# A planner's costs for TensorE and GpSimd, and the due times that go with them, replaced by another set

## The chip, the core and the metric

The kernel runs on one core of a Trainium2 chip. The metric is the time of one execution in microseconds (us) of device time. Before the change three runs gave 1165.32 us as their median (1164.49 to 1168.14).

## What is computed

Attention over 4 batches of 12 heads (448 positions, 64 numbers a head) with RMS-normalised queries and keys, then two feed-forward layers over its 1792 x 768 output, all in fp32:

```python
q_n, k_n = rmsnorm(q, g_q), rmsnorm(k, g_k)
scores = 1 / sqrt(64) * q_n @ k_n.T                  # per head
attn = exp(scores - max) / (sum + 1e-9)
x = (attn @ v) laid out as (1792, 768)
h = x @ w_in;   x = (h / (1 + exp(-h))) @ w_out      # layer 1, w_in 768 x 2048, w_out 2048 x 768
h = x @ w_in2;  x = max(h, 0) ** 2 @ w_out2          # layer 2, the same sizes
```

The inputs of the layers' weights are 8-byte floats, read as two 4-byte words each.

## The kernel before

**The work.** 24 pairs of heads go through attention one after another. Layer 1 then runs in 8 segments (two halves of the tokens, each with four quarters of the 2048 inner columns), layer 2 in 16 groups of 256 inner columns (two halves of the tokens, 8 groups each; the second half's down projection, line 1568, goes by seven products too). Each fp32 operand is split in two parts, an upper one (a rounded copy, names ending in hi) and a lower one (the difference, names ending in lo), and each product is three matmuls: upper by upper, upper by lower, lower by upper. Line 558 (`lower_part`) makes all lower parts on VectorE or GpSimd, lines 549 and 551 (`upper_part`) the upper ones on ScalarE or VectorE.

**Seven products in place of eight.** But for the first segment, whose up projection is plain (line 1017), an up projection forms 2 x 2 blocks by the scheme of seven products (`seven`, line 1104: a product is 9 matmuls of 128x448). Sums of weights are made for it at lines 1062 and 1081 (`four`), sums of activations at lines 1307 and 1253, and its results are collected from PSUM by `plus` (line 1119, VectorE). Layer 1's down projection is line 1201, its results are taken up at lines 1213 to 1221. Layer 2's down projection is lines 1443 and 1568 (sums of hidden values for it at line 1500, of weights at line 1529), its results are added at line 1462 on VectorE, and at the end of the kernel line 1620 joins the blocks. PSUM has 4 buffers "s" (down projections), 3 buffers "t" and 1 buffer "pv" (up projections).

**What sets the order.** Nothing here is issued in the order in which it is written. Every operation is recorded as a step with the engines that may do it and a time on each. A planner (class `Plan`) then plays the program: at each point it takes the step that can start first, and among those that can start at once the one with the smallest due time (`forward`). Its answer is the order of each engine's instructions and, where a step may run on several engines, the engine. Due times come from a backward pass (`backward`) plus the constants of the table `DUE`, one per kind of step and part of the program ("seg0" and "seg1" are the halves of layer 1; "end0" ends some way ahead of layer 2's second half, "end1" follows). Attention's steps stand at fixed places (`nominal`); only other work that is put between them moves. The chip follows the order, and each instruction still waits for its data by semaphore, so a wrong time in the planner makes an engine wait and never a wrong result.

The times that the change touches: `SWITCH` (line 113, added where TensorE changes between forms of matmul), `pool_t` and `any_t` (lines 475 and 478, GpSimd's time for n elements per partition), `lower_part`'s rate (line 555), four transposes (`turn_q`, line 670, and `turn_e`, line 750), attention's second product (line 807), and `PROD` (line 1040, one product of 9 matmuls). For the layers' SBUF operations a step of `any_t` may go to VectorE or GpSimd: the planner leaves it to the engine that would end it first, and it keeps two such operations from running on both engines at once (the `lock` in `forward`). An upper part (`copy_t`) may go to ScalarE or VectorE by the same rule.

Of the kernel before, what the change touches and what calls it, by code (L numbers as in the profile page):

```python
# [98 lines left out]
class Step:  # L99
# [10 lines left out]
LAG = {"pe": 0.21, "act": 0.13, "dve": 0.12, "pool": 0.12, "sp": 1.9, "none": 0.0}  # L110
SELF = {"pe": 0.0, "act": 0.1, "dve": 0.1, "pool": 0.06, "sp": 1.9, "none": 0.0}
FORM = {"scores": "rows", "attend": "columns"}
SWITCH = 0.16
ENGINES = ("pe", "act", "dve", "pool", "sp", "none")
ROUNDS = 8
AHEAD = 25.0
DUE = {
    "end0": {"acc": 4.25, "down2": -1, "h_hi": 21.25, "h_lo": 3.75, "keep_parts2": -1.25, "load_y": -0.75, "p1_copy": 3.75, "prod": 0.25, "square": 1, "u_sum": -0.5, "w_hi2": -6, "w_lo2": -0.75, "w_sum": -0.75, "y_hi": 5.25, "y_lo": 4.25, "y_sum": -3.5},
    "end1": {"acc": 2, "down2": -11.25, "h_hi": 16, "h_lo": 2.5, "h_sum": -39.5, "join": 18, "keep_parts2": -11.75, "load_parts2": -2.25, "load_word2": 1.75, "load_y": 0.5, "p1_copy": 0.5, "prod": 2, "square": 21.25, "store": -1.25, "u_sum": -1, "w_hi2": 4.25, "w_sum": -4.5, "y_lo": -3, "y_sum": 2.5},
    "now": {"ident": 5.75, "swap_pools": -0.5},  # L120
    "seg0": {"add": -0.5, "down": 3, "g_hi": 0.5, "g_lo": 0.75, "keep": 10.25, "load_raw": -6, "load_y": 0.5, "low": 1, "magnitude": -2, "merge": -6, "out1": -1, "p1_copy": 4, "part": 0.5, "prod": 4.75, "silu": 0.5, "store_y": -1, "u_sum": 2.75, "up": 2.5, "w_hi": 4.5, "w_lo": 6.25, "w_sum": -2, "y_hi": 0.75, "y_lo": 1, "y_sum": 2},
    "seg1": {"add": -4.25, "down": -4.5, "g_hi": 2.25, "g_lo": 5, "keep2": 45.25, "load_raw2": 6, "load_word": -5.5, "load_y": -0.75, "low2": -1.5, "magnitude2": -3, "merge2": -4.5, "p1_copy": -6.25, "part": -3.75, "prod": -3.25, "silu": -5.75, "store_y": 7, "u_sum": 2.25, "w_hi": 1.75, "w_lo": 1, "w_sum": -3, "y_hi": 10, "y_lo": 0.75, "y_sum": 2.5},
}


# [280 lines left out]
def kernel(  # L406
# [65 lines left out]
    def dve_t(n, rate=960.0, lock=False):  # L472
        return {"dve": (0.07 + n / rate, None, lock)}

    def pool_t(n, rate=474.0):
        return {"pool": (0.145 + n / rate, None, True)}

    def any_t(n, rate=474.0):
        return {**dve_t(n, 960.0, True), **pool_t(n, rate)}

    def copy_t(n):
# [70 lines left out]

        step(kind, when, copy_t(n), copy, reads=reads, writes=writes)

    def lower_part(kind, when, o, a, h, n, reads, writes, rate=474.0):

        step(
            kind, when, any_t(n, rate), lambda e: engine(e).tensor_tensor(o(), a(), h(), ALU.subtract),  # L558
            reads=reads, writes=writes,
        )  # L560

    def prepare(i):
# [88 lines left out]
        for n in range(2):  # L651
            n32 = sa([CP, NCH, 2, D], F32, "n")
            step(
                "norm", at, any_t(W2, 600.0),
                lambda e, n=n, n32=n32: engine(e).tensor_tensor(
                    n32.ap.rearrange("p c h d -> p h c d"),
                    qk.ap[:, n].rearrange("p (h c) d -> p h c d", h=2),
                    y.ap[:, n].rearrange("p (h c) -> p h c", h=2).unsqueeze(3).to_broadcast([CP, 2, NCH, D]),
                    ALU.mult),
                reads=[y, (qk, n)], writes=[n32],  # L660
            )
            plan.fix(i, "norm", j=n, at="dve" if i < 2 else "pool")
            pt = psum("t")

            def turn(e, n32=n32, pt=pt):
                for c in range(NCH):
                    nc.tensor.transpose(  # L667
                        pt.ap[:, c * CP:(c + 1) * CP], n32.ap[:, c].rearrange("p h d -> p (h d)"), ident.ap)

            step("turn_q", at, pe_t(0.384), turn, reads=[n32, ident], writes=[pt])  # L670
            plan.fix(i, "turn_q", j=n)

            def upper(e, n=n, pt=pt):
                o, a_ = T.ap[:, n, 0], pt.ap[:, :S]
                if n:
                    nc.scalar.activation(o, a_, AF.Copy, scale=G.ap)  # L676
                else:
                    nc.scalar.copy(o, a_)

            def lower(e, n=n, pt=pt):  # L680
                o, a_, h_ = T.ap[:, n, 1], pt.ap[:, :S], T.ap[:, n, 0].bitcast(F32)
                if n:
                    nc.vector.scalar_tensor_tensor(o, a_, G.ap, h_, ALU.mult, ALU.subtract)
                else:
                    nc.vector.tensor_tensor(o, a_, h_, ALU.subtract)

            step("q_hi", at, act_t(S, 0.08 if n else 0.0), upper, reads=[pt, G], writes=[(T, (n, 0))])
            plan.fix(i, "q_hi", j=n)
            step("q_lo", at, dve_t(S), lower, reads=[pt, G, (T, (n, 0))], writes=[(T, (n, 1))])
            plan.fix(i, "q_lo", j=n)  # L690
# [16 lines left out]
    def weigh(i, T):  # L707

        PT = [sa([CP, NB8, CT, CP], F32, "PT") for _ in range(NCH // CT)]
        sums = sb([CP, 2, NCH], F32, "sum", 3)  # L710
        for c in range(NCH):
            at = ("pair", i, c)
            E = sa([CP, 2, S], F32, "E")
            pts = [psum("s"), psum("s")]

            def scores(e, c=c, pts=pts):
                for k_, (a, b_) in enumerate(((0, 0), (0, 1), (1, 0))):
                    for j in range(2):
                        r = slice(j * D, (j + 1) * D)
                        nc.tensor.matmul(  # L720
                            pts[j].ap[:CP, :S], T.ap[r, 0, a, c * CP:(c + 1) * CP], T.ap[r, 1, b_],
                            start=(k_ == 0), stop=(k_ == 2),
                        )

            step("scores", at, pe_t(0.606), scores, reads=[(T, (n, a)) for n in range(2) for a in range(2)], writes=pts)
            plan.fix(i, "scores", c)
            for j, pt in enumerate(pts):
                mx = sa([CP, 1], F32, "mx", 6)
                step(
                    "row_max", at, {"dve": (0.535, None, False)},  # L730
                    lambda e, pt=pt, mx=mx: nc.vector.tensor_reduce(  # L731
                        mx.ap, pt.ap[:CP, :S], AX.X, ALU.max, negate=True),
                    reads=[pt], writes=[mx],
                )
                plan.fix(i, "row_max", c, j)
                step(
                    "exp", at, {"act": (0.62, None, False)},
                    lambda e, j=j, c=c, pt=pt, mx=mx, E=E: nc.scalar.activation(  # L738
                        E.ap[:, j], pt.ap[:CP, :S], AF.Exp, bias=mx.ap, accum_out=sums.ap[:, j, c:c + 1]),
                    reads=[pt, mx], writes=[(E, j), (sums, (j, c))],  # L740
                )
                plan.fix(i, "exp", c, j)
                pe = psum("t")

                def turn(e, j=j, pe=pe, E=E):
                    for m in range(NCH):
                        nc.tensor.transpose(  # L747
                            pe.ap[:CP, m * CP:(m + 1) * CP], E.ap[:, j, m * CP:(m + 1) * CP], ident.ap)

                step("turn_e", at, pe_t(0.384), turn, reads=[(E, j), ident], writes=[pe])  # L750
                plan.fix(i, "turn_e", c, j)
                copy_step(
                    "e_copy", at, ECOPY[c][j], lambda c=c, j=j: PT[c // CT].ap[:, j * NCH:(j + 1) * NCH, c % CT, :],
                    lambda pe=pe: pe.ap[:CP, :S].rearrange("p (m t) -> p m t", t=CP), S, [pe], [(PT[c // CT], (c % CT, j))],
                )
                plan.fix(i, "e_copy", c, j)
        return PT, sums

    def attend(i, vr, PT, sums):
# [32 lines left out]
        for c2, pt in enumerate(PT):  # L792

            def products(e, c2=c2, pt=pt):
                for m in range(NCH):
                    for j in range(2):
                        nc.tensor.matmul(  # L797
                            pv.ap[j * D:(j + 1) * D, c2 * CT * CP:(c2 + 1) * CT * CP],
                            vr.ap[:, j * NCH + m, :],
                            pt.ap[:, j * NCH + m].rearrange("p c t -> p (c t)"),  # L800
                            start=(m == 0),
                            stop=(m == NCH - 1),
                            skip_group_check=True,
                        )

            step(
                "attend", at, pe_t(1.456), products,
                reads=[vr] + [(pt, (c, j)) for c in range(CT) for j in range(2)], writes=[(pv, c2)],
            )
            plan.fix(i, "attend", c2)  # L810
# [226 lines left out]
    FD = 2  # L1037
    halves = {}
    W3 = HC * P
    PROD = 9 * 0.2065  # L1040

    def view(b, a, c):

# [641 lines left out]
```

## Time and profile before

| what | value |
|---|---|
| median of three runs | 1165.32 us |
| the profiled execution, its own time | 1167.08 us |
| its span, first to last instruction | 1165.3 us |
| TensorE busy | 1147.8 us (99% of the span) |
| VectorE busy | 939.3 us (81%) |
| ScalarE busy | 632.3 us (54%) |
| GpSimd busy | 287.9 us (25%), 507 instructions |
| DMA | 202 GB/s over the span |
| mean granted TensorE clock | 0.994 of 2.4 GHz |

Busy times overlap: the engines run side by side. PE is TensorE's matmuls, PEld its weight loads, DVE is VectorE, ACT ScalarE, POOL GpSimd, SP the engine that issues the DMAs. A matmul counts as busy from its start to its last result, so two that follow each other overlap, and a stream of them is read from the distance of their starts. In the chain of waits (the work that ended last, followed back from the last instruction) the time of a piece of TensorE's work is therefore also the time that the stream took.

### The profile page before, as it was taken

Reading aid. Unit: us, or ns where it says so; the run is one execution under the profiler, and the core shown is the slowest. Engines: PE = TensorE matmul, PEld = TensorE weight load, DVE = VectorE, ACT = ScalarE, POOL = GpSimd, SP = SyncE. Lnnn points to the kernel's source line nnn. Section 1 sums busy time; section 2 is a strip of 40 time slices with the busy share of each in tenths; the row PEclk is TensorE's granted clock in tenths of the full one; section 3 lists DMA queues with packets and bytes.
Section 4 is the critical chain, followed back from the end, with each engine's and each line's share of the span. In section 5 each row is a group of like instructions: output and inputs, shape, how many; then the busy total and the mean of one; then the engine's idle time right before and its main releaser. Section 6 shows DMA issues by size and latency. Waiting matters only on the chain.

```text
span 1165.3 us, 19244 instructions
## 1 busy us (share of the span) xinstructions
PE 1147.8 (99%) x6817; PEld 1018.8 (87%) x6817; DVE 939.3 (81%) x1685; ACT 632.3 (54%) x1290; POOL 287.9 (25%) x507
## 2 busy tenths in 40 slices
PE   7999999998999999999999999999999999999998
PEld 5777777777999999999999999999998999999997
DVE  7888888886876868996878698588888976888876
ACT  5999999985554444555535353543433535333321
POOL 4566676632000101210111021001121120122220
PEclk8999999999999999999999999999999999999999
DMA  6566768578855564778776849977777696555444
GB/s 175 94 103 115 105 109 111 99 125 175 275 167 185 172 212 133 263 236 273 244 238 209 272 145 329 337 271 261 286 264 260 217 378 230 177 176 190 164 163 135
DMA packets 142064, 235.22 MB, mean 202 GB/s; under 512 B 32016, under 2 KB 105744, under 8 KB 141968
## 3 DMA queue, kind: packets, MB, share of 16 engines
q1 hardware_dynamic: 141728, 233.80, 67.2%
q8 instruction: 54, 0.88, 0.3%
q14 instruction: 42, 0.34, 0.1%
q10 hardware_dynamic: 240, 0.20, 0.1%
HBM read 157.58 MB, written 76.37 MB: 201 GB/s over the span
## 4 chain that ended last, share of the span: by engine, by line
PE 91%; DVE 4%; ACT 2%; DMA 1%; issue 1%; SPq 0%; POOL 0%; ACTq 0%; DVEq 0%; POOLq 0%
PE t L1104 22%; PE s L1201 20%; PE s L1443 11%; PE pv L1104 9%; PE t L747 7%; PE pv L797 7%; PE s L720 6%; PE s L1568 6%; PE t L1017 2%; PE t L667 2%; DMA raw<-in_moe_w_out_dram 1%; DVE gg L1462 1%; DVE w L558 1%; DVE g L1119 0%; DVE g L1500 0%
## 5 line engine op out<-in xcount | busy, mean ns | idle before, releaser
L1201 PE MATMUL s<-gg,w 128*128 128x448 f32 x1152 | 240.4, 367 | 0.0
L1201 PEld LDWEIGHTS s<-gg,w 128*128 128x128 f32 x1152 | 216.2, 188 | 19.8 <-DVE g L1213 0.3
L1119 DVE TENSOR_TENSOR g<-t,g 128x448 f32<-128x448 f32 x180 | 108.8, 619 | 63.9 <-PE t L1104 53.1
L1443 PE MATMUL s<-w,gh 128*128 128x384 f32 (+1 forms) x564 | 143.0, 334 | 2.1 <-DVE gg L1462 1.1
L738 ACT ACTIVATE E<-s,mx 112x448 f32<-112x448 f32 x192 | 122.9, 653 | 13.7 <-ACT xf L537 7.9
L731 DVE TENSOR_REDUCE mx<-s 112x1 f32<-112x448 f32 x192 | 107.4, 611 | 14.4 <-PE s L720 14.1
L1462 DVE TENSOR_TENSOR gg<-s,gg 128x384 f32<-128x384 f32 (+1 forms) x197 | 102.6, 547 | 18.1 <-PE s L1443 17.7
L558 DVE TENSOR_TENSOR w<-W,w 128x768 fp32r<-128x768 f32 (+1 forms) x123 | 111.7, 917 | 4.2 <-ACT w L549 3.3
L1443 PEld LDWEIGHTS s<-w,gh 128*128 128x128 f32 x564 | 101.8, 188 | 4.0 <-DVE gg L1462 1.9
L1104 PE MATMUL t<-yb,w 128*128 128x448 f32 x468 | 103.1, 367 | 0.2 <-DVE w L558 0.2
L747 PEld LDWEIGHTS t<-ident,E 112*112 112x112 f32 x768 | 73.8, 134 | 32.5 <-issue 19.1
L549 ACT CAST w<-W 128x768 fp32r<-128x768 f32 (+1 forms) x74 | 54.9, 744 | 83.8 <-PE s L1201 31.9
L747 PE MATMUL t<-ident,E 112*112 112x112 f32 x768 | 94.7, 266 | 1.2 <-ACT E L738 1.2
L1368 ACT ACTIVATE g<-g 128x448 f32<-128x448 f32 x48 | 27.7, 578 | 124.6 <-DVE g L1119 124.1
L1443 PE MATMUL s<-w,gl 128*128 128x384 f32 (+1 forms) x282 | 94.3, 335 | 0.3 <-POOL gl L558 0.3
L1104 PEld LDWEIGHTS t<-yb,w 128*128 128x128 f32 x468 | 87.6, 188 | 8.1 <-DVE w L558 0.5
L797 PE MATMUL pv<-PT,vv 112*64 112x224 f32 x768 | 83.0, 359 | 0.1
L720 PE MATMUL s<-T 64*112 64x448 f32 x576 | 73.8, 388 | 1.3 <-ACT T L676 1.2
L1104 PE MATMUL pv<-xb,w 128*128 128x448 f32 x324 | 72.4, 367 | 0.0
L539 DVE COPY PT<-t 112x448 f32<-112x448 f32 x96 | 59.1, 618 | 11.6 <-PE t L747 11.5
L797 PEld LDWEIGHTS pv<-PT,vv 112*64 112x64 f32 x768 | 51.0, 136 | 20.0 <-ACT xf L537 0.3
L1104 PEld LDWEIGHTS pv<-xb,w 128*128 128x128 f32 x324 | 60.7, 188 | 5.5
(168 smaller groups left out, 2213.1 us busy)
## 6 DMA issues: line engine op xcount, KB each, us to landing
raw<-in_moe_w_in_dram SPq DMA_DIRECT2D x32, 768.0 KB
raw<-in_moe_w_out_dram SPq DMA_DIRECT2D x24, 512.0 KB
raw<-in_moe_w_out_dram SPq DMA_DIRECT2D x16, 768.0 KB
su<-w SPq DMA_DIRECT2D x16, 768.0 KB
w<-su SPq DMA_DIRECT2D x16, 768.0 KB
xf<-y SPq DMA_DIRECT2D x48, 224.0 KB
xf<-x SPq DMA_DIRECT2D x39, 224.0 KB
ki<-W SPq DMA_DIRECT2D x16, 384.0 KB
```

The source lines that it names most:

```text
L558: kind, when, any_t(n, rate), lambda e: engine(e).tensor_tensor(o(), a(), h(), ALU.subtract),
L720: nc.tensor.matmul(pts[j].ap[:CP, :S], T.ap[r, 0, a, c * CP:(c + 1) * CP], T.ap[r, 1, b_], start=(k_ == 0), stop=(k_ == 2),)
L731: lambda e, pt=pt, mx=mx: nc.vector.tensor_reduce(mx.ap, pt.ap[:CP, :S], AX.X, ALU.max, negate=True),
L738: lambda e, j=j, c=c, pt=pt, mx=mx, E=E: nc.scalar.activation(E.ap[:, j], pt.ap[:CP, :S], AF.Exp, bias=mx.ap, accum_out=sums.ap[:, j, c:c ...
L747: nc.tensor.transpose(pe.ap[:CP, m * CP:(m + 1) * CP], E.ap[:, j, m * CP:(m + 1) * CP], ident.ap)
L797: nc.tensor.matmul(pv.ap[j * D:(j + 1) * D, c2 * CT * CP:(c2 + 1) * CT * CP], vr.ap[:, j * NCH + m, :], pt.ap[:, j * NCH + m].rearrange("p ...
L1104: nc.tensor.matmul(pt.ap[:, :S], w_()[:, c0 + c, :], view(b, a, c)(), start=(start and c == 0 and k == 0), stop=(c == HC - 1 and k == 2), ...
L1119: lambda e: nc.vector.tensor_tensor(o.ap, pt.ap[:, :S], a.ap, ALU.add),
L1201: nc.tensor.matmul(pt.ap[:, :S], w_()[:, f, :], gg.ap[:, k, a, f, :], start=(f == 0 and n == 0), stop=(f == HQ - 1 and n == 2),)
L1443: nc.tensor.matmul(pt.ap[:, :en], g.ap[:, fi, c0:c0 + P], w_()[:, 0, e0:e0 + en], start=(n == 0), stop=(n == 5),)
L1462: "acc", at, dve_t(n), lambda e: nc.vector.tensor_tensor(o(), pt.ap[:, :n], o(), ALU.add),
L1568: nc.tensor.matmul(pt.ap[:, :NH], a[i][0](m), b[j][0](), start=(start and k == 0), stop=(k == 2), skip_group_check=True,)
```

## The change

Six times of the planner are changed, and the table `DUE` is replaced as a whole; nothing else differs. No operation is added or left out. The numbers of instructions on TensorE (6435) and of DMAs stay; some steps that have a choice move between VectorE, ScalarE and GpSimd.

```diff
-SWITCH = 0.16
+SWITCH = 0.13
...
-    "end0": {"acc": 4.25, "down2": -1, "h_hi": 21.25, "h_lo": 3.75, ...
+    "end0": {"down2": -1.5, "h_hi": 50.5, "h_lo": -0.75, "keep_parts2": 4.25, ...
...
-    def pool_t(n, rate=474.0):
-        return {"pool": (0.145 + n / rate, None, True)}
-
-    def any_t(n, rate=474.0):
+    def pool_t(n, rate=415.0):
+        return {"pool": (0.1 + n / rate, None, True)}
+
+    def any_t(n, rate=415.0):
...
-    def lower_part(kind, when, o, a, h, n, reads, writes, rate=474.0):
+    def lower_part(kind, when, o, a, h, n, reads, writes, rate=415.0):
...
-            step("turn_q", at, pe_t(0.384), turn, reads=[n32, ident], writes=[pt])
+            step("turn_q", at, pe_t(0.406), turn, reads=[n32, ident], writes=[pt])
...
-                step("turn_e", at, pe_t(0.384), turn, reads=[(E, j), ident], writes=[pe])
+                step("turn_e", at, pe_t(0.406), turn, reads=[(E, j), ident], writes=[pe])
...
-                "attend", at, pe_t(1.456), products,
+                "attend", at, pe_t(1.512), products,
...
-    PROD = 9 * 0.2065
+    PROD = 9 * 0.2028
```

How the order moves, at three places. Over the whole program GpSimd has 19 instructions fewer (512 to 493), VectorE 6 more, ScalarE 13 more; among the moved ones are 9 upper parts of weights (128x768) that go from VectorE to ScalarE. TensorE's order is the same up to the end of the first segment's up projection.

**ScalarE, at the end of attention.** W and raw are a weight tile and the 8-byte words that it is made from (lines 920 and 925 read raw), g<-t at line 1029 is the first SiLU of layer 1, which empties a buffer "t" of PSUM. Before:

```order
L537 COPY xf<-pv 128x448
L920 ACTIVATE W<-raw 128x512
L925 ACTIVATE raw<-raw 128x512
L1029 ACT_TABLE_LOAD
L1029 ACTIVATE g<-t 128x448
L549 CAST gg<-g 128x448
L549 CAST w<-W 128x512
L1029 ACTIVATE g<-t 128x448
```

Now:

```order
L537 COPY xf<-pv 128x448
L549 CAST w<-W 128x768
L920 ACTIVATE W<-raw 128x512
L925 ACTIVATE raw<-raw 128x512
L1029 ACT_TABLE_LOAD
L1029 ACTIVATE g<-t 128x448 x2
L549 CAST gg<-g 128x448
L920 ACTIVATE W<-raw 128x512
```

An upper part of weights has come ahead, and the second SiLU follows the first at once. The two reads of raw still stand ahead of the first SiLU.

**TensorE, where the fourth segment's down projection meets the next up projection.** s<-gg is the down projection, t and pv are products of the up projection with the activations yb, xb, xc, gh. Before:

```order
L1201 MATMUL s<-gg,w 128x448 x12
L1104 MATMUL t<-yb,w 128x448 x18
L1104 MATMUL t<-xb,v 128x448 x9
L1201 MATMUL s<-gg,w 128x448 x24
L1104 MATMUL pv<-xb,w 128x448 x9
L1104 MATMUL t<-xc,w 128x448 x9
L1104 MATMUL t<-xb,w 128x448 x9
L1104 MATMUL t<-yb,w 128x448 x9
```

Now:

```order
L1201 MATMUL s<-gg,w 128x448 x144
L1104 MATMUL pv<-gh,w 128x448 x2
...
L1104 MATMUL t<-yb,w 128x448 x18
L1104 MATMUL t<-xb,v 128x448 x9
L1104 MATMUL pv<-xb,w 128x448 x9
L1104 MATMUL t<-xc,w 128x448 x9
L1104 MATMUL t<-xb,w 128x448 x9
```

All 144 matmuls of the down projection now stand ahead of the next segment's first product; before, 24 of them stood between its fourth and its fifth product.

**GpSimd, in layer 2's first half.** gl is a lower part of the hidden values, v and w<-W are lower parts of weights, xf a sum of activations; the numbers count buffers in the order in which the planner issues them. Before:

```order
L558 TENSOR_TENSOR gl_10288<-g_10233,gh_10251 128x448
L558 TENSOR_TENSOR gl_10288<-g_10263,gh_10251 128x448
L558 TENSOR_TENSOR v_10311<-W_10267,v_10311 128x384
L558 TENSOR_TENSOR w_10324<-W_10308,w_10324 128x768
L558 TENSOR_TENSOR gl_10549<-g_10530,gh_10534 128x448
L1253 TENSOR_TENSOR xf_10757<-xf_10757,xf_10772 128x448
L558 TENSOR_TENSOR gl_10851<-g_10828,gh_10833 128x448
```

Now:

```order
L558 TENSOR_TENSOR gl_10006<-g_9822,gh_9993 128x448
L558 TENSOR_TENSOR w_10103<-W_9887,w_10103 128x768
L558 TENSOR_TENSOR w_10333<-W_10307,w_10333 128x768
L558 TENSOR_TENSOR yb_10584<-xf_10070,yb_10584 128x448
L1253 TENSOR_TENSOR xf_10757<-xf_10757,xf_10771 128x448
```

Of four operations that stood together around buffer number 10300 one is left, and a second lower part of 128x768 has come. From the first to the last matmul of layer 2's first half GpSimd has 15 of these operations where it had 27.

## Rows read from the trace of the kernel before

**Rows 1.** The page: the span, busy time by engine, and the chain by engine.

```profile
span 1165.3 us, 19244 instructions
...
PE 1147.8 (99%) x6817; PEld 1018.8 (87%) x6817; DVE 939.3 (81%) x1685; ACT 632.3 (54%) x1290; POOL 287.9 (25%) x507
...
PE 91%; DVE 4%; ACT 2%; DMA 1%; issue 1%; SPq 0%; POOL 0%; ACTq 0%; DVEq 0%; POOLq 0%
```

**Rows 2.** Weight loads' waits, whole span: waited for, us in total, times, longest.

```profile
PEld t L1017 <- ACT g L1029: 3.4, 1, 3.4
```

**Rows 3.** The chain of waits, 262 to 290 us: start, us, what.

```profile
269.79 10.34 DMA raw<-in_moe_w_out_dram
...
282.71 0.55 ACT g L1029
...
283.31 6.72 PE t L1017 x24
```

**Rows 4.** Stretches of 2 us: busy time by engine, PEclk is the granted clock.

```profile
284.00:286.00 2.00, 2.00 (x8) 1.81 (x8) 2.00 (x3) 1.63 (x3) 1.22 (x1) 0.67 1.06 386
286.00:288.00 2.00, 2.00 (x7) 1.74 (x7) 2.00 (x5) 0.56 (x1) 0.00 (x0) 0.50 1.07 284
```

**Rows 5.** The chain of waits, whole span: two streams of 126 matmuls.

```profile
306.78 26.04 PE s L1201 x126
...
583.30 25.53 PE s L1201 x126
```

**Rows 6.** Two stretches of layer 1, in order PE, PEld, DVE, ACT, POOL, clock.

```profile
288.50:511.50 223.00, 223.00 (x1081) 202.52 (x1080) 181.61 (x313) 110.65 (x185) 20.31 (x14) 1.00 0.64 202
515.00:735.00 220.00, 220.00 (x1087) 203.59 (x1086) 170.73 (x284) 107.37 (x170) 30.74 (x22) 1.00 0.75 250
```

**Rows 7.** Weight loads' waits, 288 to 735 us.

```profile
PEld s L1201 <- DVE g L1213: 0.3, 1, 0.3
PEld t L1104 <- DVE g L1119: 0.2, 1, 0.2
```

**Rows 8.** Weight loads' waits, 735 to 990 us.

```profile
PEld s L1443 <- DVE gg L1462: 1.9, 2, 1.5
PEld s L1568 <- DVE part L558: 1.8, 2, 1.1
PEld s L1443 <- POOL gl L558: 0.6, 1, 0.6
PEld t L1104 <- DVE w L558: 0.5, 1, 0.5
PEld pv L1104 <- DVE w L558: 0.5, 1, 0.5
```

**Rows 9.** The timeline of POOL and of DVE around 879 us.

```profile
878.24 1.83 POOL L558 TENSOR_TENSOR w<-W,w 128x768 fp32r<-128x768 f32 x1 [0.35 <-ACT w L549]
...
876.46 0.55 DVE L1062 TENSOR_TENSOR W<-W 128x384 f32<-128x384 f32 x1
...
878.29 2.20 DVE L1081 TENSOR_TENSOR W<-W 128x384 f32<-128x384 f32 x1
```

**Rows 10.** The timeline of PE there, with the idle time before and its releaser.

```profile
881.01 0.61 PE L1443 MATMUL s<-w,gh 128*128 128x384 f32 x2 [1.13 <-DVE gg L1462]
```

**Rows 11.** Layer 2's first half as one stretch.

```profile
735.00:960.00 225.00, 223.09 (x1183) 211.91 (x1182) 183.15 (x306) 94.92 (x168) 36.56 (x27) 1.00 0.77 280
```

**Rows 12.** Groups by line and shape: upper parts of 128x768 on DVE and on ACT.

```profile
L551 DVE CAST w<-W 128x768 fp32r<-128x768 f32 x43 | 26.4, 614 | 9.2 <-PE pv L1104 4.1 <-PE s L1201 4.0
...
L549 ACT CAST w<-W 128x768 fp32r<-128x768 f32 x43 | 35.9, 834 | 57.0 <-PE s L1201 18.0 <-DVE W L1081 12.6 <-PE s L1443 9.4
```

**Rows 13.** Weight loads' waits, 990 us to the end.

```profile
PEld s L1443 <- DVE gh L551: 1.2, 1, 1.2
PEld s L1568 <- ACT part L549: 1.1, 4, 0.3
```

**Rows 14.** The last piece of the chain of waits.

```profile
1161.65 0.36 DVE gg L1462
```

More of the change, by code (lines that the diff above doesn't have):

```diff
@@ L117 @@
 DUE = {
-    "end0": {"acc": 4.25, "down2": -1, "h_hi": 21.25, "h_lo": 3.75, "keep_parts2": -1.25, "load_y": -0.75, "p1_copy": 3.75, "prod": 0.25, "square": 1, "u_sum": -0.5, "w_hi2": -6, "w_lo2": -0.75, "w_sum": -0.75, "y_hi": 5.25, "y_lo": 4.25, "y_sum": -3.5},
-    "end1": {"acc": 2, "down2": -11.25, "h_hi": 16, "h_lo": 2.5, "h_sum": -39.5, "join": 18, "keep_parts2": -11.75, "load_parts2": -2.25, "load_word2": 1.75, "load_y": 0.5, "p1_copy": 0.5, "prod": 2, "square": 21.25, "store": -1.25, "u_sum": -1, "w_hi2": 4.25, "w_sum": -4.5, "y_lo": -3, "y_sum": 2.5},
@@ L120 @@
-    "now": {"ident": 5.75, "swap_pools": -0.5},
-    "seg0": {"add": -0.5, "down": 3, "g_hi": 0.5, "g_lo": 0.75, "keep": 10.25, "load_raw": -6, "load_y": 0.5, "low": 1, "magnitude": -2, "merge": -6, "out1": -1, "p1_copy": 4, "part": 0.5, "prod": 4.75, "silu": 0.5, "store_y": -1, "u_sum": 2.75, "up": 2.5, "w_hi": 4.5, "w_lo": 6.25, "w_sum": -2, "y_hi": 0.75, "y_lo": 1, "y_sum": 2},
-    "seg1": {"add": -4.25, "down": -4.5, "g_hi": 2.25, "g_lo": 5, "keep2": 45.25, "load_raw2": 6, "load_word": -5.5, "load_y": -0.75, "low2": -1.5, "magnitude2": -3, "merge2": -4.5, "p1_copy": -6.25, "part": -3.75, "prod": -3.25, "silu": -5.75, "store_y": 7, "u_sum": 2.25, "w_hi": 1.75, "w_lo": 1, "w_sum": -3, "y_hi": 10, "y_lo": 0.75, "y_sum": 2.5},
+    "end0": {"down2": -1.5, "h_hi": 50.5, "h_lo": -0.75, "keep_parts2": 4.25, "load_y": -0.25, "prod": -0.75, "relu": 2.25, "square": -8.25, "u_sum": 5.25, "w_hi2": 0.25, "w_lo2": 1.25, "w_sum": -3.75, "y_hi": 1.5, "y_lo": -0.75, "y_sum": -2.75},
@@ new lines @@
+    "end1": {"acc": 2, "h_hi": 39.25, "h_lo": 7.5, "h_sum": -6.25, "join": 5.5, "load_parts2": 0.5, "load_word2": -6.5, "load_y": 0.5, "p1_copy": -0.25, "prod": 47.25, "relu": -2.5, "square": 0.5, "store": -2.75, "u_sum": 7.25, "w_hi2": -1, "w_lo2": -0.25, "w_sum": -4.5, "y_hi": 0.5, "y_lo": 13.5, "y_sum": 0.25},
+    "now": {"ident": 12.75},
+    "seg0": {"add": -5, "down": -0.5, "g_hi": -0.75, "g_lo": 2, "load_raw": -0.5, "load_y": 4.5, "low": 3.75, "magnitude": -0.75, "merge": -2, "out1": 2.5, "p1_copy": 2.75, "part": -0.25, "prod": -0.25, "silu": -8.5, "store_y": 4, "u_sum": -3.25, "up": -1.75, "w_hi": -0.25, "w_lo": 0.25, "w_sum": -0.75, "y_hi": 1.75, "y_lo": -6},
@@ L123 @@
+    "seg1": {"add": -11.25, "down": -1.75, "g_hi": 1, "g_lo": 6.25, "keep2": 58.5, "load_raw2": 3, "low2": 21, "magnitude2": 8, "merge2": -5.75, "out1": -42.25, "p1_copy": -1.5, "part": 1, "silu": -1.5, "store_y": -15, "u_sum": 0.25, "w_hi": 4.75, "w_lo": 1, "y_hi": 5.75},
 }
```

## The prediction

> **What bounds the kernel now.** I read the page first: TensorE is busy for 99% of the span, and 91% of the chain of work that ended last is its own [rows 1]. So the time is TensorE's stream plus its holes, and a saving on another engine counts only where it ends a hole. The holes stand in the list of the weight loads' waits. A weight load goes ahead of its matmul, so it shows a wait in full, where the matmul before it still counts as busy. Behind attention there is one of 3.4 us [rows 2]. In the 447 us from 288 to 735, which are nearly the whole of layer 1, two lines make 0.5 us [rows 7]. In layer 2's first half five lines make 5.3 us (1.9 + 1.8 + 0.6 + 0.5 + 0.5; three of 0.2 to 0.3 us are not shown) [rows 8]. In its second half the two largest lines make 2.3 us [rows 13]. Last I read what the stream itself runs at: 126 matmuls of 128x448 take 26.04 us at 307 us and 25.53 us at 583 us [rows 5], which is 206.7 ns from one start to the next and then 202.6 ns, though the granted clock is 1.00 of 2.4 GHz in both stretches [rows 6]. With about a thousand matmuls in each half of layer 1 that is as large as all waits of layer 2's first half.
>
> The number of TensorE's instructions is the same after the change, so five places carry the sum.
>
> **The hole behind attention: 0.** TensorE stands still because the first SiLU, which empties a buffer of PSUM, is queued on ScalarE behind two reads of raw, and raw lands 10.34 us after its issue at 269.79 us; the SiLU ends at 283.26 us and TensorE goes on at 283.31 us [rows 3]. Then the granted clock is 0.67 and 0.50 for two stretches of 2 us, with 8 and 7 matmuls in them [rows 4], where 206.7 ns apart there would be 9.7 in each: 4.4 matmuls or 0.9 us more. In the new order the two reads still stand ahead of the first SiLU. The upper part that has come in front of them lies in the time in which ScalarE waits for the DMA, so that covers it; if it fell behind the landing it would cost its 0.83 us [rows 12]. The second SiLU, now earlier, was not what TensorE waited for. I take 0, with ends 0 and +0.8 us; nothing in the order brings the DMA forward, so there is no gain.
>
> **The spacing in layer 1: 0.** The short spacing begins where TensorE waits at 512 us, for VectorE's g at line 1119 (0.2 us) [rows 7]. From 288.5 to 511.5 us there are 1081 matmuls, from 515 to 735 us 1087 [rows 6]. The difference is (26.04 - 25.53) / 126 = 4.0 ns a matmul. Were the spacing short from the start, the first stretch would lose 1081 x 4.0 ns = 4.3 us; were it long to the end, the second would gain 1087 x 4.0 ns = 4.4 us. At 512 us stands the segment boundary of the second order piece. There 24 down matmuls, 24 x 206.7 ns = 5.0 us of time for VectorE between the fourth and the fifth product, have gone, and stand ahead of the first product instead. VectorE has as much to do for the same five products as before, so I take it that TensorE waits there again and the spacing changes in the same place: 0, with ends -4.3 and +4.4 us.
>
> [...]
>
> **Layer 2's first half: -2.4 us.** The longest wait shows how it comes about. At 878.24 us GpSimd begins a lower part of 128x768, 1.83 us long; VectorE's sum of weights at line 1081 begins at 878.29 us and takes 2.20 us, where the like sum at line 1062 took 0.55 us two microseconds earlier [rows 9]. Behind it on VectorE is the addition that empties a buffer "s", and TensorE stands for 1.13 us until 881.01 us for that addition [rows 10]. GpSimd's 27 operations in this half took 36.56 us [rows 11], 1.35 us each. The new order has 15, so 15 x 1.35 = 20.3 us, 44% less time in which VectorE can be held. VectorE takes over most of the 12: at 0.55 us [rows 9] they are 6.6 us. Against that 9 of its upper parts go to ScalarE, 9 x 0.614 = 5.5 us (over the whole program), where they take 9 x 0.834 = 7.5 us [rows 12]; ScalarE is busy for 94.92 of 225 us here [rows 11] and covers them. So VectorE's own work stays about where it is, 183.15 of 225 us [rows 11]. I let the 5.3 us of waits go down with GpSimd's time: 5.3 x 44% = 2.4 us. The ends are all 5.3 us gone, and +1.5 us, since two lower parts of 128x768 now stand where one did and the one cost a wait of 1.5 us [rows 8]. The nearest row for a taken away crowd is that same one, so I stay between.
>
> The Trainium skill (SBUF — State Buffer, section Who interferes with whom) says that a VectorE instruction with two SBUF inputs and a GpSimd instruction that reads SBUF block each other for the whole instruction, and that a VectorE instruction with at most one SBUF input, outside its two-port modes, is not touched. The sum of weights in rows 9 agrees: it has two SBUF inputs and ends only after GpSimd has. By that rule 12 operations fewer free up to 12 x 1.35 = 16 us of VectorE, more than there is to gain, and the term would be -5.3 us; that is the second rival.
>
> **Layer 2's second half and the end: 0.** The order of the repeated groups differs by two lower parts of sums that now stand together. The four waits for ScalarE's upper part, 1.1 us [rows 13], have the same work ahead of them: 0, with 0.5 us either way. The last group waits 1.2 us for an upper part that VectorE does behind the joins of line 1620 [rows 13]. VectorE has 12 joins where it had 10, GpSimd 3 where it had 5: 2 x 0.55 = 1.1 us more on VectorE, about as much less holding by GpSimd; 0, with 1 us either way. The last addition starts at 1161.65 us [rows 14], right behind the last matmul, in both orders: 0.
>
> **The sum.** The profiled execution took 1167.08 us, 1.8 us of it outside its span of 1165.3 us, and the sum is 1167.08 - 2.4 = 1164.7 us. The median of the runs, 1165.32 us, is 1.76 us lower, so the forecast for a median is 1162.9 us. By its own ends (-5.3 to +1.5 in layer 2's first half, less than 1 us elsewhere) it runs from 1160.0 to 1166.8 us.
>
> **Rivals.** All against 1165.3 us.
>
> - *The spacing is short early.* If TensorE has to wait once soon after 288 us, most of 4.3 us comes off: with the -2.4 us that is 1158.6 us. For it: one wait of 0.2 us was enough. Against it: TensorE was busy for 223.00 of 223 us there [rows 6], in much the same order.
> - *VectorE is freed altogether* in layer 2's first half: 1165.3 - 5.3 = 1160.0 us. Against it: GpSimd keeps 15 operations, two of them of the longest kind.
> - *The spacing stays long: slower.* Its place is the segment boundary at 512 us, its price +4.4 us less the 0.5 us of waits: 1169.2 us, or 1166.8 us if layer 2 gains its 2.4 us. It decides on whether TensorE waits at all there. The 144 down matmuls that now stand together give VectorE 144 x 206.7 ns = 29.8 us ahead of the first product; if it is done with all five products' weights by then, no wait comes.
> - *GpSimd's two long operations* meet VectorE in a full stretch each, and the joins cost their 1.1 us: +2.6 us, 1167.9 us. Against it: the crowd of four is gone.
> - *The change does nothing*: the order is another, the waits as long in other places: 1165.3 us.
>
> **How the numbers follow.** The forecast 0.35; short early 0.18; freed altogether 0.12; long spacing 0.20, half of it with layer 2's gain and half without; the two long operations 0.10; nothing 0.05. A measurement of this kernel tells 0.3% from no change, which is 3.5 us: faster lies under 1161.8 us, slower over 1168.8 us. Faster: the first two rivals (0.30) and the lower end of the forecast (0.06), 0.36. Slower: the half of the long spacing without a gain (0.10), and 0.07 for the upper ends of the last two. The rest, 0.47, is within. The range from 1158.0 to 1169.0 us leaves out the two faster rivals together (1155.7 us, some 0.07) and the upper ends (some 0.12).
>
> **What would show it.** Right: again one wait of about 3.4 us at the first SiLU; streams of 126 matmuls that take 26.0 us in the first half of layer 1 and 25.5 us in the second; some 3 us of weight loads' waits in layer 2's first half, with GpSimd busy for about 20 us in it; 1.2 us before the last down projection. Wrong: a first half of layer 1 at 25.5 us for 126, a second half at 26.0 us, waits in layer 2's first half of 5 us or more, or a wait in layer 1 longer than 1 us.

## The result and the profile after

The changed kernel is slower. Its median is 1174.03 us over seven runs (1171.05 to 1178.45 us), against 1165.32 us for the kernel before on the same chip; the ratio of the two is 1.0069, 95% interval 1.0043 to 1.0094. The forecast was 1162.9 us, and the range ended at 1169.0 us.

The page of the changed kernel, span and busy time by engine, as [rows 1]:

```profile
span 1170.1 us, 19245 instructions
...
PE 1145.8 (98%) x6817; PEld 1020.9 (87%) x6817; DVE 944.4 (81%) x1691; ACT 639.6 (55%) x1303; POOL 262.4 (22%) x488
```

GpSimd lost 25 us of work and VectorE gained 5, as the order said, and TensorE, with 6817 matmuls in the profile of either kernel, stands still for longer. The profiled execution took 1172.03 us, 1.9 us outside its span; the spans differ by 4.8 us. To see where, I divided both traces at the first matmul of lines 1017, 1443 and 1568 (us):

| stretch | before | after | difference |
|---|---|---|---|
| up to the first up-projection | 270.75 | 270.30 | -0.45 |
| up-projection behind attention and layer 1 | 465.81 | 467.53 | +1.72 |
| layer 2's first half | 222.30 | 220.55 | -1.75 |
| layer 2's second half and the end | 206.44 | 211.74 | +5.30 |

The +1.7 us is a sum of things that work against each other. The hole behind attention, the weight loads' waits as in [rows 2], 270 to 288 us:

```profile
PEld t L1017 <- ACT g L1029: 4.0, 1, 4.0
```

The stretches behind it, as [rows 4]; the last columns are PEclk, DMA share and GB/s:

```profile
284.00:286.00 2.00, 2.00 (x7) 1.76 (x6) 2.00 (x4) 1.57 (x3) 0.35 (x1) 0.50 1.06 396
286.00:288.00 2.00, 2.00 (x7) 1.79 (x6) 1.57 (x4) 0.16 (x1) 0.00 (x0) 0.50 1.05 218
288.00:290.00 2.00, 2.00 (x7) 1.78 (x7) 0.47 (x1) 0.00 (x0) 1.15 (x1) 0.60 1.07 356
```

The hole is 0.6 us longer, and the half clock lasts to 289.6 us and not to 288.1 us: 1.8 us together, by the start of the same matmul behind both. Then the spacing. The same 180 us of layer 1, in which TensorE never stops in either kernel, before and after:

```profile
290.00:470.00 180.00, 180.00 (x873) 163.47 (x872) 143.11 (x245) 88.30 (x146) 9.99 (x7) 1.00 0.61 191
```

```profile
290.00:470.00 180.00, 180.00 (x890) 166.84 (x890) 142.06 (x237) 95.65 (x160) 12.61 (x10) 1.00 0.60 192
```

17 matmuls more, or 3.5 us: the changed kernel has the short spacing from 290 us on, where before had the long one until 512 us. Over that whole stretch it is the 4.3 us that the prediction priced for this case. Against it stand new waits. Weight loads of the changed kernel, 288 to 735 us, where [rows 7] had 0.5 us:

```profile
PEld s L1201 <- DVE g L1213: 2.4, 3, 1.2
PEld s L1201 <- DVE w L558: 1.4, 1, 1.4
PEld s L1201 <- DVE gg L558: 1.2, 2, 0.9
PEld t L1104 <- DVE w L558: 0.4, 1, 0.4
```

By the distances of matmul starts, TensorE stands for 4.5 us at these seven waits and stood for 0.3 us before: 4.2 us more, and 1.8 - 4.3 + 4.2 is the +1.7 us.

In layer 2's first half GpSimd's work went down as counted (36.56 us in [rows 11], now 21.68 us), and no wait is left before 920 us, where [rows 8] had its longest at 880 us. As one stretch, and the weight loads' longest waits from 735 to 990 us:

```profile
735.00:960.00 225.00, 224.05 (x1192) 213.60 (x1191) 183.38 (x319) 97.15 (x172) 21.68 (x15) 1.00 0.78 280
```

```profile
PEld s L1568 <- ACT gg L1459: 1.3, 1, 1.3
PEld pv L1104 <- ACT g L1374: 1.1, 1, 1.1
PEld s L1568 <- ACT part L549: 1.1, 1, 1.1
```

Line 1568 is the second half's down projection, which begins at 958.4 us here and at 958.9 us before. So of these three only the wait for `g` stands in the first half, at its end; the one for `gg` at 961 us is the second half's, and it was 0.2 us before. ScalarE's timeline shows why it grew: two upper parts of `part` stand ahead of the copy of line 1459 that TensorE needs.

```profile
959.19 0.51 ACT L549 CAST part<-g 128x384 fp32r<-128x384 f32 x1 [0.35 <-DVE g L1500]
...
960.35 0.49 ACT L549 CAST part<-g 128x384 fp32r<-128x384 f32 x1
...
961.83 1.62 ACT L1459 COPY gg<-s 128x384 f32<-128x384 f32 x4
```

The largest item is the second half. Weight loads' waits, 990 us to the end, where [rows 13] had 1.2 and 1.1 us:

```profile
PEld s L1568 <- DVE part L558: 6.8, 6, 1.8
PEld s L1443 <- DVE gh L551: 0.9, 1, 0.9
```

Six waits, one in each repeated group. One group in the timelines of VectorE, GpSimd and TensorE, changed kernel:

```profile
1071.81 0.55 DVE L1462 TENSOR_TENSOR gg<-s,gg 128x384 f32<-128x384 f32 x1
1072.28 1.49 DVE L558 TENSOR_TENSOR part<-g,part 128x384 fp32r<-128x384 f32 x1
...
1072.20 1.15 POOL L558 TENSOR_TENSOR gl<-g,gh 128x448 fp32r<-128x448 f32 x1 [1.78 <-ACT gh L549]
...
1073.82 1.51 PE L1568 MATMUL s<-xb,part 128*128 128x384 f32 x7 [0.68 <-DVE part L558]
```

The same group in the kernel before:

```profile
1068.39 0.55 DVE L558 TENSOR_TENSOR part<-g,part 128x384 fp32r<-128x384 f32 x1
1068.86 0.55 DVE L1462 TENSOR_TENSOR gg<-s,gg 128x384 f32<-128x384 f32 x1
1069.33 1.04 DVE L1500 TENSOR_TENSOR g<-g 128x384 f32<-128x384 f32 x1
...
1068.79 1.17 POOL L558 TENSOR_TENSOR gl<-g,gh 128x448 fp32r<-128x448 f32 x1 [1.78 <-ACT gh L549]
```

The operation on `part` is the lower part of the sum S1 (`put("S1", ...)`, line 1511), which TensorE needs for the fifth product. Before, it began 0.40 us ahead of GpSimd's lower part of `gl`; the operation that GpSimd then held was the sum of line 1500 (1.04 us), for which TensorE does not wait. In the new order the addition of line 1462 stands in front of S1's lower part, which now begins 0.08 us behind GpSimd's start, takes 1.49 us for 0.55 us, and TensorE stands. In all six groups it begins 0.07 to 0.14 us behind GpSimd and takes 1.43 to 1.49 us. The addition reads one input from PSUM and is not held (0.55 us, inside GpSimd's 1.17 us).

### The profile page after: what moved, and what is told of

Same layout as the page of the kernel before. It is cut to its first block, busy times and chain, and to the rows that moved or that the text cites. A ratio compares the mean times of both kernels' runs of the same rounds, so it can differ in the third digit from the quotient of the medians.

```text
span 1170.1 us, 19245 instructions
## 1 busy us (share of the span) xinstructions
PE 1145.8 (98%) x6817; PEld 1020.9 (87%) x6817; DVE 944.4 (81%) x1691; ACT 639.6 (55%) x1303; POOL 262.4 (22%) x488
## 4 chain that ended last, share of the span: by engine, by line
PE 89%; DVE 7%; DMA 2%; ACT 1%; issue 1%; SPq 0%; DVEq 0%; ACTq 0%
PE t L1104 22%; PE s L1201 18%; PE s L1443 12%; PE pv L1104 8%; PE t L747 8%; PE pv L797 7%; PE s L720 6%; PE s L1568 6%; PE t L1017 2%; PE t L667 2%; DVE gg L1462 1%; DMA raw<-in_moe_w_out_dram 1%; DVE g L1119 1%; DVE part L558 1%; DVE w L558 1%
## 5 line engine op out<-in xcount | busy, mean ns | idle before, releaser
L558 DVE TENSOR_TENSOR w<-W,w 128x768 fp32r<-128x768 f32 (+1 forms) x124 | 108.4, 880 | 2.2 <-ACT w L549 0.9
L549 ACT CAST w<-W 128x768 fp32r<-128x768 f32 (+1 forms) x87 | 65.0, 749 | 82.1 <-PE s L1201 30.8
```

## The experiments

The theory from the traces: the loss is VectorE's operations with two SBUF inputs held by GpSimd's at places where TensorE waits for them, six times in layer 2's second half (5.3 us) and some seven times in layer 1. Its rivals are that VectorE simply has too much to do there, and that the difference is the spacing's or the half clock's. All experiments but the extra stop of TensorE edit the planner's answer, in `Plan.issue`, so that nothing else is planned anew; `resort` keeps the order but for the steps named, each put behind another, by their numbers (comments in the excerpts of code are added here, and "..." stands for lines left out):

```diff
-        self.span, start, at, order = self.schedule()
+        self.span, start, at, order = rearrange(self, *self.schedule())
```

Three groups ran, each beside the kernel before on one chip: its medians there were 1162.57, 1163.10 and 1162.19 us, and ratios are to these.

**The changed kernel again** (no edit).

> The changed kernel once more, unchanged. Theory: the spacing of TensorE's matmuls behind the half-clock stretch is settled anew in each execution, so this profile may show either 202.7 ns or 206.7 ns from 290 us to the first wait at about 476 us, and the time scatters by about 3.7 us (918 matmuls x 4.0 ns); median 1174 us. The waits of 0.85 us in each group of layer 2's second half come back at the same places (6.8 us in all). Rival: the spacing belongs to the order, so it is 202.7 ns again and the scatter has another source.

Median 1170.09 us, ratio 1.0060 (1.0038 to 1.0083): the result repeats. In this profile the hole is 2.2 us and no half clock follows it, and the spacing is again short to 476 us. The seven waits of layer 1 stand in the same places (5.1 us), and the six of the second half too, one of 1.8 us at 985 us and five of 1.0 us. A half-clock stretch came instead behind the first of these:

```profile
989.00:991.00 2.00, 2.00 (x8) 2.00 (x7) 1.20 (x3) 0.00 (x0) 0.37 (x1) 0.50 0.00 0
```

**S1's lower part ahead of the addition**, as before (`swap_lower`).

```diff
+        if getattr(s, "tag", "") == "S1" and at[s.n] == "dve":   # S1's lower part, at place k
...
+            if plan.steps[order[p]].kind == "acc" and not any(t.n in order[p:k] for t in s.needs):
+                order.insert(p, order.pop(k))   # p: the place of VectorE's step before it
```

> VectorE does the lower part of S1 ahead of the addition of line 1462 in front of it, in each of the six groups of layer 2's second half, as in the kernel before; nothing else is moved. Theory (the lower part starts 73 ns behind a GpSimd operation of 1.15 us and is held to its end): without the meeting the six waits of 0.85 us go, 5.1 us, so 1174.0 - 5.1 = 1168.9 us. Rival (VectorE is simply full in this stretch, the wait only moves to the addition or to the sum behind it): within 1 us of the changed kernel, 1173 to 1175 us.

Median 1166.07 us, ratio 1.0019 (0.9998 to 1.0040): 4.0 us less than the changed kernel. Its weight loads' waits, 990 us to the end, and the group in the timelines:

```profile
PEld s L1568 <- ACT part L549: 1.7, 6, 0.3
PEld s L1568 <- DVE gg L1462: 1.2, 5, 0.3
```

```profile
1068.14 0.55 DVE L558 TENSOR_TENSOR part<-g,part 128x384 fp32r<-128x384 f32 x1
1068.61 0.55 DVE L1462 TENSOR_TENSOR gg<-s,gg 128x384 f32<-128x384 f32 x1
1069.08 1.04 DVE L558 TENSOR_TENSOR part<-g,part 128x384 fp32r<-128x384 f32 x1
...
1068.53 1.18 POOL L558 TENSOR_TENSOR gl<-g,gh 128x448 fp32r<-128x448 f32 x1 [1.77 <-ACT gh L549]
```

S1's lower part is 0.55 us again. Now the one of S3 is held (1.04 us), and TensorE needs that one later. The theory holds, 1 us smaller than put: the short waits in the first of these views, 2.9 us, were hidden behind the long ones in the changed kernel. By the profile the second half takes 208.61 us, 3.1 us less than in the changed kernel and still 2.2 us more than before; the wait for line 1459 at the start of the half stays, at 1.3 us.

**The same order, GpSimd's operation taken away** (`gl_dve`): the lower part of `gl` goes to VectorE, behind S3's lower part.

```diff
+            at[n] = "dve"                 # n: gl's lower part, in six groups
+            moves.append((n, s.n))        # s: S3's lower part
```

> VectorE's order of S1's lower part stays as changed, but GpSimd's lower part of 128x448 that it meets is done on VectorE, behind S3's lower part, in the six groups. Theory (holding by GpSimd): the lower part of S1 takes 0.55 us and not 1.49 us, the six waits go, 5.1 us less, though VectorE has 6 x 0.53 = 3.2 us more to do: 1169 us. Rival (the addition put in front of the lower part makes it late, 0.47 us each, GpSimd or not): waits of about half the length stay, 1171 to 1172 us. Second rival (VectorE is full): slower, 1177 us.

Median 1166.33 us, ratio 1.0021 (1.0005 to 1.0038). VectorE's timeline, where the two lower parts behind each other now take 1.02 us together:

```profile
1069.52 0.55 DVE L1462 TENSOR_TENSOR gg<-s,gg 128x384 f32<-128x384 f32 x1
1069.98 1.02 DVE L558 TENSOR_TENSOR part<-g,part 128x384 fp32r<-128x384 f32 x2
1070.92 0.62 DVE L558 TENSOR_TENSOR gl<-g,gh 128x448 fp32r<-128x448 f32 x1
```

This tells the holding from the order: the addition is still in front of S1's lower part and VectorE has more to do, and the six waits are gone all the same, for nearly the same gain as the swap. (The second half takes 209.66 us in this profile, and the wait for line 1459 stays here too, at 1.3 us.) The first rival would have left half of the waits (1171 us), the second would have made it slower.

**The first SiLUs ahead of the reads of raw** (`silu_first`).

```diff
+    return span, start, at, resort(plan, order, ((1913, 1858), (1914, 1858)))   # L920, L925 behind the second SiLU
```

> On ScalarE the first two SiLUs stand ahead of the two reads of the first raw of w_out; nothing else is moved on purpose. Theory (TensorE stands only because the first SiLU is queued behind reads that wait for the DMA): the hole of 4.0 us goes, and with it the half-clock stretch of 17 matmuls, 17 x (373 - 203) ns = 2.9 us; 6 to 7 us less, 1167 to 1168 us. Rival (the spacing behind it is then the long one, 206.7 ns, as no stop precedes it): 3.7 us of that are given back until 476 us, 1171 us. Second rival (the table load or the weights of w_out, now read later, make a new wait): the hole only moves, 1174 us.

Median 1168.18 us, ratio 1.0046 (1.0028 to 1.0064): 1.9 us less than the changed kernel by the medians, though the two intervals overlap. ScalarE's timeline, and the clock near 990 us:

```profile
279.03 0.55 ACT L1029 ACTIVATE g<-t 128x448 f32<-128x448 f32 x1 [5.50 <-PE t L1017]
280.27 0.55 ACT L1029 ACTIVATE g<-t 128x448 f32<-128x448 f32 x1 [0.69 <-PE t L1017]
280.71 0.66 ACT L920 ACTIVATE W<-raw 128x512 f32<-128x512 f32 x1
```

```profile
989.00:991.00 2.00, 2.00 (x8) 2.00 (x8) 1.27 (x3) 0.32 (x1) 1.01 (x1) 0.52 0.00 0
```

The hole is gone, so the queue on ScalarE was its cause. Two things took most of it back: the spacing was the long one for the next 1006 matmuls (to 479 us), as the first rival said, and the half-clock stretch came behind the stops at 985 us.

**One stop of TensorE on purpose** (`spacing_wait`, from the kernel before): a copy on ScalarE of a strip of the weights, onto itself, between two matmuls that read it.

```diff
+            nc.scalar.copy(wh()[:, 3:5, :8], wh()[:, 3:5, :8].bitcast(F32))
```

> The kernel before, with one copy of 16 numbers onto themselves on ScalarE between two matmuls of layer 1's up-projection at about 295 us; TensorE reads what is copied, so it has to stop there once, for about 0.5 us. Theory (a stop of TensorE sets the spacing of the matmuls that follow to the short one, until a run of matmuls of another width): 202.7 ns from 295 us on in the profile, where before showed 206.7 ns up to 512 us; executions with the long spacing lose 1040 x 4.0 ns - 0.5 us = 3.7 us, the others gain 0.5 us, so the median goes from 1162.6 to about 1161 us and the upper heap of times (1165 to 1166 us) thins out. Rival (the spacing is settled by the order or by the half-clock stretch alone): 206.7 ns stay in the profile and the median rises by 0.5 us, 1163 us.

Median 1162.65 us, ratio 0.9993 (0.9973 to 1.0013): no effect, and the theory of it falls. The timeline of TensorE, from the first stream behind attention on:

```profile
274.48 5.03 PE L1017 MATMUL t<-xb,w 128*128 128x448 f32 x24
...
302.06 3.37 PE L1017 MATMUL t<-xb,w 128*128 128x448 f32 x15 [0.29 <-ACT w L1691]
...
308.37 26.20 PE L1201 MATMUL s<-gg,w 128*128 128x448 f32 x126
```

and the first stream in the kernel before:

```profile
275.19 5.12 PE L1017 MATMUL t<-xb,w 128*128 128x448 f32 x24
```

The instructions up to there are the same in both, and one execution has the short spacing (5.03 us) and the other the long one (5.12 us). Behind the stop the spacing turned from 202.7 ns to 206.7 ns and stayed so for 1022 matmuls; the stop made it longer. So a stop draws the spacing anew, and either may come.

**Both, from the kernel before** (`silu_wait_b`): the SiLUs first, and the stop.

> The kernel before with both: ScalarE does the first two SiLUs ahead of the two reads of the first raw of w_out, and the one stop of TensorE at about 295 us. Theory: the hole of 2 to 4 us goes and with it the half-clock stretch (1.5 us), and the long spacing that then follows (seen without a stop) lasts only from 270 to 295 us: 1162.6 - 3.4 - 1.5 + 0.5 = 1158 us, or 1156 us where the kernel before had the long spacing. Rival (the half-clock stretch is due whatever happens and only moves, as one at 987 us did): 1159 to 1160 us. Second rival (the first SiLU was never the bound): 1163 us.

Median 1163.03 us, ratio 0.9998 (0.9978 to 1.0017): the second rival's number, for another reason. In its profile the hole and the half clock are gone (1.2 us of short waits for the SiLUs in their place), and the stop is again followed by 1022 matmuls at 206.7 ns, 4.1 us more than at the short spacing.

**Layer 1's operations off GpSimd** (`to_dve`).

```diff
+    for n in (2485, 2562, 2565, 2628, 3331, 3354, 3349):
...
+        at[n] = "dve"
```

> Seven of GpSimd's operations of layer 1 that overlap with VectorE's ahead of TensorE's seven waits (six lower parts and one sum) are done on VectorE at the same places. Theory (VectorE is held there by GpSimd): each holding cost 0.9 us, the same work costs VectorE 0.55 us, so the waits of 5.2 us in layer 1 become 1 to 3 us: 2 to 4 us less, 1166 to 1168 us. Rival (VectorE has too much queued ahead of the additions that empty the buffers, from the order): the waits stay or grow by 7 x 0.55 us: 1170 to 1173 us.

Median 1169.57 us, ratio 1.0061 (1.0040 to 1.0082): as the changed kernel. Its waits, 288 to 735 us:

```profile
PEld s L1201 <- DVE gg L558: 1.4, 1, 1.4
PEld s L1201 <- DVE w L558: 0.4, 1, 0.4
PEld s L1201 <- DVE g L1213: 0.4, 1, 0.4
```

5.1 us have become 2.2 us, as the theory had it, so the holding is shown in the trace; in the time it is not, and a gain of 3 us is no more than the two intervals leave open. What is left is not the holding by these seven: the wait for `gg` is 1.4 us here and was 0.7 us at the same place in the second profile of the changed kernel. This profile ran at the long spacing for 980 matmuls (281 to 484 us). Whether that goes with the missing stops or was drawn by chance is open.

**Layer 2 in the order of before** (`l2_before`): the steps of stage "end" take order and engine from a table of numbers of the kernel before.

> Attention and layer 1 in the changed order, layer 2 in the order of before (its steps' order and engines from a table of numbers). Theory (layer 2 costs 5.3 - 1.7 = 3.6 us of the loss, attention and layer 1 the rest): 1170.1 - 3.6 = 1166.5 us. Rival (all of the loss is layer 2's): 1162.6 us, as the kernel before. Second rival (layer 1 or the hole holds it all): 1170 us.

Median 1181.33 us, ratio 1.0157 (1.0127 to 1.0187), against all three. The two orders do not fit where they meet: weight loads' waits, 690 to 990 us,

```profile
PEld s L1201 <- DVE g L1213: 5.1, 2, 3.2
PEld s L1443 <- DVE gg L1462: 3.0, 4, 1.5
PEld s L1443 <- ACT gh L549: 2.5, 1, 2.5
```

so its total tells nothing on the change. Behind the seam it is clean: the second half takes 206.42 us, as in the kernel before (206.44 us), and 5.3 us less than in the changed one, with all that goes before it different.

**Both places mended** (`swap_to_dve`: the swap and the seven operations), **and the SiLUs first** (`best_a`).

> The changed kernel with both places mended: S1's lower part ahead of the addition in the six groups, and the seven operations of layer 1 on VectorE and not on GpSimd. Theory (these two kinds of meeting are the whole loss): 4.0 us (measured for the swap alone) and up to 2.9 us (the waits that went in layer 1's trace) off 1170.1 us: 1163 to 1166 us, within 3 us of the kernel before. Rival (the stops of layer 1 are worth nothing, since the spacing drawn anew behind each takes as much as it gives): 1166 us, as the swap alone. Second rival (something else in the changed order costs the rest): 1168 us.

> As the last, and ScalarE does the first two SiLUs ahead of the two reads of the first raw. Theory (three independent holes, each worth what it was alone, 4.0, 0 to 2.9 and 1.9 us): 1161 to 1164 us, at or just under the kernel before. Rival (without the hole the half-clock stretch comes elsewhere and the long spacing lasts from 270 us on): no gain over the kernel without it, 1163 to 1166 us.

Medians 1164.92 us, ratio 1.0018 (0.9999 to 1.0038), and 1159.95 us, ratio 0.9984 (0.9965 to 1.0002). The first is no better than the swap alone (1.0019), so again layer 1's mending is seen in its waits (2.7 us for 5.1 us) and not in the time. With the SiLUs first, a kernel in the changed order is level with the one before or just under it; there was no half clock between 250 and 1155 us in that profile.

**The kernel before, SiLUs first** (`silu_first_b`), **and without the crowd at 880 us** (`best_b`).

```diff
+    at[3900] = "dve"        # the lower part of 128x768 of rows 9
+    return span, start, at, resort(plan, order, ((1913, 1858), (1914, 1858), (3900, 3878)))
```

> The kernel before with the first two SiLUs ahead of the two reads of the first raw, without the extra stop. Theory: the hole (3.4 us) and its half-clock stretch (1.5 us) go, less 1.2 us of short waits that the trace with the extra stop showed in their place: 1163 - 3.5 = 1159 to 1160 us. Rival (as in the changed kernel, where 1.9 us was all that came of it): 1161 us. Second rival (nothing, as with the extra stop): 1163 us.

> As the last, and the lower part of 128x768 that holds VectorE's sum of weights at 878 us (rows 9) is done on VectorE some eight additions later. Theory: the waits of 1.5 + 0.5 us at 880 us go as well, at 0.5 us for the longer operation: 1.5 us under the last, 1158 us. Rival (another wait takes its place, as VectorE is busy there): no difference to the last.

Medians 1160.76 us, ratio 0.9992 (0.9974 to 1.0010), and 1158.58 us, ratio 0.9968 (0.9947 to 0.9989). `best_b` is faster than both kernels: 3.6 us under the one before, some 11 us under the changed one. Its hole behind attention:

```profile
PEld t L1017 <- ACT g L1029: 0.4, 1, 0.4
```

with two more short ones up to 300 us, 1.6 us in all; layer 2's first half takes 220.65 us, 1.6 us less than before and as little as in the changed kernel: one operation moved off GpSimd gave what there was to gain there. Not all of it stays: TensorE now waits 1.5 us for line 1459 at the start of the second half (0.6 us in `silu_first_b`), and the two halves together are 0.5 us shorter than in that profile. The medians of the two differ by 2.2 us, which their intervals do not separate.

## Why the prediction was wrong

- **Layer 2's second half and the end: 0, with 0.5 us either way.** This step failed; it measured +5.3 us. "The order of the repeated groups differs by two lower parts of sums that now stand together" was the right difference, and it was passed over because each operation was priced by its length and not by what runs on GpSimd at its new start. The trace of before had the answer, in the four groups that run like the one shown: S1's lower part begins at 1068.39 us, an addition behind which it goes costs 0.47 us of VectorE (1068.86 to 1069.33 us), so it would begin at 1068.86 us, 0.07 us behind GpSimd's 1068.79 us. Held to 1069.96 us and 0.42 us longer (1073.77 us against 1073.35 us in the changed trace), it ends some 1.4 us later than before. At the six waits TensorE stands for 5.8 us, by the distances of matmul starts (0.84 us at each of five, 1.6 us at the first), and two kernels without them are 4.0 and 3.8 us faster by their medians. A second item is in the same stretch, the wait for line 1459 at 961 us (1.3 us for 0.2 us), from ScalarE's new order and not from the holding; both of those kernels keep it, and no run took away it alone. Against the two, some 1.9 us of before's short waits are gone.
- **The spacing in layer 1: 0, with -4.3 and +4.4 us.** The lower end came in the profile, and not for the reason given. The text tied the spacing to the stop at 512 us; the runs show that it can change at any stop, and either value with the same instructions ahead of it. So the term belongs to the execution and not to the change. It is one source of the scatter of every kernel here (1157.47 to 1169.53 us for the kernel before in the three groups).
- **New waits in layer 1.** The prediction had no term for them: it took VectorE's work as the same and saw only 27 against 15 GpSimd operations of layer 2. 4.2 us of standing are new. The longer waits have a meeting of two operations ahead of them, such as this one (GpSimd, VectorE, TensorE; changed kernel); `to_dve` took more than half of them out of the trace, but what they cost in time stays open:

```profile
484.56 1.48 POOL L558 TENSOR_TENSOR yb<-xf,yb 128x448 fp32r<-128x448 f32 x1 [3.30 <-ACT yb L549]
...
484.94 1.58 DVE L1307 TENSOR_TENSOR xf<-xf 128x448 f32<-128x448 f32 x1
...
487.11 1.08 PE L1201 MATMUL s<-gg,w 128*128 128x448 f32 x4 [0.87 <-DVE g L1213]
```

- **The hole behind attention: 0.** Right as a term. It was 3.4 and 4.9 us in two executions of before's order, 4.0 and 2.2 us in two of the changed one, so nothing shows that the 0.6 us of the profiles and the longer half clock are the change's. The cause given (SiLU queued behind the reads of raw) is shown by `silu_first`. The half clock behind the hole was read too low, at 0.9 us: 13 matmuls, and not 15, start between 284 and 288 us, which is 1.3 us.
- **Layer 2's first half: -2.4 us.** Right in kind, -1.7 us in size, and the size was off by a misreading: the 1.8 us of line 1568 in [rows 8] lie behind the first matmul of the second half (958.9 us), so the first half had 3.5 us of the 5.3 us, and 44% of that is 1.5 us. The waits at 880 us went, and one for ScalarE's `g` (1.1 us) came at the half's end. `best_b` shows that most of the old loss hung on one operation.
- **The sum.** -0.45 + 1.72 - 1.75 + 5.30 = 4.8 us between the profiles. The medians differ by 8.7 us, 7.5 us in the second comparison. Without what varies between executions of one order (the spacing, the hole and its half clock) the profiles leave 4.2 - 1.7 + 5.3 = 7.8 us: the profile of before had drawn the long spacing, that of the changed kernel the short one, and this hid 4 us. That the rest of the runs drew both alike is not shown.
- **The rivals.** The one that ended slower put the price on the spacing. The true one, S1's lower part pushed behind GpSimd's start, stood in none.

The planner did know the rule: it keeps two such operations of VectorE and GpSimd apart, and its plan has `gl`'s lower part behind both of the sums' lower parts. But only the order on each engine is carried to the chip. GpSimd has nothing queued ahead of `gl` and starts 0.08 us after ScalarE's upper part is there (1072.12 us), whatever VectorE is about to do.

The Trainium skill (SBUF — State Buffer, section Who interferes with whom) says that a VectorE instruction with two SBUF inputs and a GpSimd instruction that reads SBUF block each other, and that one with at most one SBUF input, outside its two-port modes, is not touched. The groups above agree in both halves: S1's lower part took 1.49 us, the addition with one input in PSUM 0.55 us beside the same operation of GpSimd. The prediction used the rule only where it promised a gain.

## What to carry to other kernels

When an operation is moved by one place, add the length of what now stands in front of it to its old start and look at what the other engines are doing at that moment; a shift of half a microsecond decided who held whom, six times over. An order that is planned anew can lose time at more than one place: here two upper parts ahead of a copy on ScalarE also cost a wait of 1.3 us where the second half begins. A table that orders each engine's own queue does not order engines against each other, so a plan's "behind" holds only if a wait or the queue itself makes it so. Differences under half a per cent need several profiles: here the kernel before ran some 960 matmuls of layer 1 at 206.7 ns and `silu_first_b` the same ones at 202.7 ns, 4 us apart, and TensorE waited in neither.

## What the runs showed of the hardware

- Matmuls of 128x448 on 128x128 run at 202.7 or at 206.7 ns from start to start, at a granted clock of 1.00. In fourteen profiles the first stream behind attention is long nine times and short five; in before's order three of five are short. The value mostly holds until TensorE stops, over a thousand matmuls; in layer 2, between the runs of 128x384, it was about 206.5 ns in every profile.
- The half clock (granted 0.5, that is 1.2 GHz) came behind the hole at 280 us in seven profiles, with holes of 2.8 to 4.9 us. Where it did not (holes of 2.2 and 2.9 us, and none in `silu_first`), it came at 987 us, behind two stops of 0.9 and 1.6 us; in `best_a`, which has no hole and 0.5 us for the second of these, in neither place.
- The holding goes both ways: a lower part of 128x512 on GpSimd, 1.30 us elsewhere, took 4.19 us in the changed kernel while VectorE ran one operation with two SBUF inputs behind another:

```profile
475.50 4.19 POOL L558 TENSOR_TENSOR w<-W,w 128x512 fp32r<-128x512 f32 x1 [3.64 <-ACT w L549]
```
